# Top-k attention with a feed-forward block: ReLUs of the mask moved to the head of a step, GpSimd's work reordered, more units transposed by VectorE

## The chip, the core and the metric

One core of a Trainium2 chip runs the whole program in one launch. The metric is the device time of that launch in microseconds. Engines are named as in the profile: PE is TensorE (matmuls; PEld are its weight loads), DVE is VectorE, ACT is ScalarE, POOL is GpSimd, SP is SyncE, which issues the DMAs here. Each engine executes its own instructions strictly in the order in which the program has them, and waits on the others by semaphores.

## The reference

```python
# q, k, v: (B=8, H=8, S=576, D=64), float32
scores = q @ k.transpose(0, 1, 3, 2) / 8
kth = np.partition(scores, -32, axis=-1)[..., -32:-31]      # 32nd largest of each row
scores = np.where(scores >= kth, scores, -1e9)
attn = np.exp(scores - scores.max(-1, keepdims=True))
attn = attn / (attn.sum(-1, keepdims=True) + 1e-9)
x = (attn @ v).transpose(0, 2, 1, 3).reshape(8, 576, 512)   # heads side by side

xn = (x - x.mean(-1)) / sqrt(x.var(-1) + 1e-6) * g_ln
out = x + np.maximum(xn @ w_ch1, 0.0) @ w_ch2               # 512 -> 2048 -> 512
```

The two feed-forward weights arrive as 8-byte numbers and are turned into float32 by the kernel itself.

## The kernel before

**Units.** Heads are taken in pairs. For a batch and a head pair, the 576 queries are cut into four tiles of 128 and a rest of 64. A *unit* is one such tile for both heads: two halves of 128 x 576 scores, or, for the rest, one (64 rows of each head). There are 160 units, 20 for each of the 8 batches; 128 are whole, 32 are rests. A *group* is a run of units of one head pair whose products with the values are made together: from batch 2 on, tiles 0, 1 and the rest, then tiles 2 and 3.

**Steps.** The program's main loop has one step for each unit (and a few more at the end). In step `n` it works on several units at once, each at another stage:

- PE makes the scores of unit `n+2` into four PSUM banks (two halves of the keys for two heads, L402), and ACT copies them to SBUF (`scores`, L383, four copies).
- DVE *halves* unit `n+1` at the end of the step (`halve`, L423 and L424: maximum and minimum of the left and right half of a row), so that the top values are sought among 288 columns.
- DVE *selects* in unit `n` (`select`, in four parts): MAX8 finds the 8 largest of each row (L445, L437), MATCH_REPLACE8 takes them out (L431), four times. The eighth value of the fourth time is the threshold.
- For unit `n-1` the mask is made: ACT scales the threshold and the row's maximum (`prepare`, L457 and L458), a very steep ReLU gives a large number where the score is below the threshold (`mask`, L494), POOL subtracts the score from it (L497), and ACT takes Exp with the negative scale and sums the row (`weigh`, L505).
- For unit `n-2` the weights are transposed, so that keys lie on partitions. A *moved* unit goes by DVE: two transposes in 32 x 32 blocks into the unit's score tile (`move`, L536), one DMA to HBM (L551) and, in step `n` = unit + 3, four DMAs back that put the blocks in place (`bring`, L546). Other units go by PE: four transposes for each half (L563), copied out by ACT (L575). The last 64 keys of both heads, the *end keys*, are always transposed by PE (`turn_ends`, L596), for a moved unit in step unit + 3, and copied by ACT (L606).
- Two to four steps behind its last unit, a group is multiplied with the values (`values`, L629 and L636).

**Feed-forward.** When the rows of a batch are ready, a *block* of 256 rows is given to a list of PE work: transposes, hidden layer (L776), projection (L933; the first block's at L815). `fill()`, called some eight times a step, takes as much from that list as the step's share allows; the share is worked out so that a block is finished when the next is given. ACT evacuates (L799, L898, L907), POOL makes sums of the hidden parts (L863 to L869) and of outputs (L913, L917, L747). These run some `fill()` calls later (`sums_later`, `ends_later`, `stores`).

**Weights.** In steps 0 to 20 the weights are converted in 32 pieces, some beforehand, one per step up to step 9, then two: `fetch` (a DMA), `split` (ACT makes magnitude, low part and sign, L163, L165, L168; POOL clamps the magnitude, L164), `shift` (DVE, L176), `join` (POOL, L182 and L184). Up to step 8 a piece is split in the middle of its step; later ones at the end of the step (`weights(n, 1)`). Shift and join come one step later, at its end. After the first block, POOL forms sums of parts of the second weight in four steps (`form_pair`, L987 to L990).

**Watch.** POOL also notes for each unit how far the threshold is from a bound (`watch`, L464), which tells at the end whether a second, slower pass is needed. It reads the unit's halved scores, of which there are two buffers.

**Buffers.** PSUM has two pools: five banks for scores, transposes and products with values, three for the feed-forward. There are five score tiles in SBUF, and two for the masked scores `e`: the ReLU of unit `n-1` writes the one that unit `n-3` had, whose end keys PE must have transposed.

The order on every engine is the order of the calls in the loop; nothing is rearranged.

Of the kernel before, what the change touches and what calls it, by code (L numbers as in the profile page):

```python
# [29 lines left out]
def compute(  # L30
# [31 lines left out]
    HALF = S // 2  # L62
# [35 lines left out]
    def turned():  # L98
        return brief("tp")
# [110 lines left out]
    def weights(n, phase):  # L210

        now, before = batches.get(n, []), batches.get(n - 1, [])
        coming = batches.get(n + 1, [])
        if phase == 0:
            for x in coming if n < LATE else []:
                x.fetch()
            for x in now[0::2] if n < LATE else []:
                x.split()  # L220
        elif phase == 1:
            for x in before:
                x.shift()
            for x in before:
                x.join()
            for x in now if n >= LATE else now[1::2]:
                x.split()
            for x in coming if n >= LATE else []:
                x.fetch()

    todo = []
    share = [0.0]
# [143 lines left out]

    def scores(u):

        u.sc = scpool.tile([P, 2, S], FP32, tag="sc", name="sc")
        made = [score_half(u, s) for s in range(2)]  # L380
        for t in range(len(u.tiles)):
            for s in range(2):
                nc.scalar.copy(  # L383
                    u.sc[:, t, s * HALF : (s + 1) * HALF], made[s][t][:, 0:HALF]
                )

    def score_half(u, s):
# [195 lines left out]
        heads = () if u.moved else range(len(u.tiles))  # L583
        return [lambda t=t: part(t) for t in heads] + [last]

    def turn_ends(u):

        q0 = place_of(u) * 32
        g = u.group
        ps = turned()  # L590
        if u.rest:
            nc.tensor.transpose(ps[0:R, 0:P], u.e[:, 0, JP:S], ident[:])
            nc.tensor.transpose(ps[:, P : 2 * P], u.e[:, 0, JP - R : S], ident[:])
        else:
            ends_e = u.e[:].rearrange("p t n -> p (t n)")[:, JP : JP + P]
            nc.tensor.transpose(ps[:, 0:P], ends_e, ident[:])  # L596

        def copy():
            if u.rest:
                for h in range(2):  # L600
                    nc.scalar.copy(  # L601
                        g.pt[h * R : (h + 1) * R, 2 * J, q0 : q0 + R],
                        ps[h * R : (h + 1) * R, h * (P + R) : h * (P + R) + R],
                    )
            else:
                nc.scalar.copy(g.pt[:, 2 * J, q0 : q0 + P], ps[:, 0:P])  # L606

        return copy
# [443 lines left out]
    CONVERTING = max(n for n in batches if batches[n]) + 2  # L1052
    EARLY = jobs[NHP].first

    for u in units[EARLY:]:
        u.moved = not u.rest and u is not u.group.units[-1]


    for j, after_j in zip(jobs, jobs[1:] + [None]):
# [43 lines left out]
    def at(i):  # L1103
        return units[i] if 0 <= i < N else None
# [94 lines left out]
    nc.sync.dma_start(grow[:], g_ln.rearrange("(c p) -> c p", p=P))  # L1199
    load(fresh[1], nc.sync, nc.scalar)  # L1200
    scores(units[0])
    halve(units[0])
    scores(units[1])
    load_gain()
    weights(-1, 0)
    weights(-1, 1)
    for n in range(END):
# [20 lines left out]
        if quick:  # L1228
            values(g)
            take_values(g)  # L1230
        for x in ahead:
            scores(x)
        if g and not quick:
            values(g)
        if n in brings:
# [14 lines left out]
        if doubt is not None and at(n - 2) and at(n - 2).ends_watch:  # L1250
            settle_watch(at(n - 2).half)
            if n == N + 1:
                tell()
        if early:
            prepare(ex)
            for t in range(2):
                mask(ex, t)
            weights(n, 0)
            for t in range(2):
                weigh(ex, t)  # L1260
        if not early:
            weights(n, 0)
        fill()
        turned_before = at(n - 3)
        if turned_before and turned_before.moved:
            late_ends = turn_ends(turned_before)
        if mk and not early:
            prepare(mk)
            mask(mk, 0)
        fill()  # L1270
        if mk and len(mk.tiles) > 1 and not early:
            mask(mk, 1)
        if g and not quick:
            take_values(g)
        if late_ends:
# [17 lines left out]
                load(fresh[later], nc.sync, nc.sync, n >= EARLY)  # L1293
        if n == 0:
            scores(units[2])
        for x in (u if n < EARLY else None, mk if n > EARLY else None):
            if x and x is units[x.job.last]:
                load_values(x.job)
                ends_due[n + 1] = x.job
# [33 lines left out]
        fill()  # L1333
        if u:
            select(u, 3)
            if doubt is not None:
                watch(u)
        if nxt:
            halve(nxt)
        weights(n, 1)  # L1340
        if g and not quick and g.job.hp == NHP - 1:
            for qt in g.qts:
                if qt < J:
                    arrived(n, (g.job.b, qt), xs[g.job.b, qt])
        if plain_done[0] is not None and plain_done[0] < n:
            if made_pair:
                keep_pair(made_pair.pop())
            if pairs_left:
                made_pair.append(form_pair(pairs_left.pop(0)))
        if late and late.job.hp == NHP - 1:  # L1350
            r = late.job.b // 2
            if r % 2:
# [61 lines left out]
```

## Time and profile before

| | us |
|---|---|
| median of three runs | 1620.12 |
| lowest and highest | 1617.61, 1620.48 |
| the profiled execution | 1619.01 |
| its span, first to last instruction | 1617.1 |

| engine | busy us | share of the span |
|---|---|---|
| PE (PEld beside it) | 1482.7 (1119.5) | 92% (69%) |
| DVE | 1411.5 | 87% |
| ACT | 1072.8 | 66% |
| POOL | 1071.2 | 66% |

The profile is of one execution. It lists busy time by engine and in 40 equal slices (each digit is the busy share in tenths, 9 is 90% or more), groups of instructions by line with their mean duration and the idle time ahead of them, waits ("A <- B" is idle time of A that B's end ended; then the total, how often, and the longest), and the chain of waits, which is followed back from the last instruction. A timeline row has the start, the duration and, in brackets, the idle time ahead and what ended it. A busy PE is not one at its peak, since the ends of matmuls are modelled.

### The profile page before, as it was taken

The page shows a single profiled execution, that of the slowest core. Times are in us where ns is not written, and L with a number is a line of the kernel's source. Part 1 is how long each engine was busy: PE and PEld are TensorE (multiplying, and loading weights), DVE is VectorE, ACT ScalarE, POOL GpSimd, SP SyncE. Part 2 cuts the span into 40 slices and gives each one's busy share as a digit, 9 for nine tenths or more (in the row PEclk, how much of TensorE's full clock was granted, in tenths as well). Part 3 has the DMA queues.
Part 4 walks back from the last instruction along what each step waited for, and adds up shares of the span by engine and source line. Part 5 has one row for each costly group of instructions (what it writes and reads, how often), then busy time and mean ns, then how long its engine had stood idle before and what let it go on. Part 6 is the DMA issues. An engine that isn't in the chain of part 4 may idle for free.

```text
span 1617.1 us, 27069 instructions
## 1 busy us (share of the span) xinstructions
PE 1482.7 (92%) x7770; PEld 1119.5 (69%) x7770; DVE 1411.5 (87%) x3971; ACT 1072.8 (66%) x2984; POOL 1071.2 (66%) x1489
## 2 busy tenths in 40 slices
PE   3568778699979999999999999999999999999997
PEld 1336446467757677777777777777777777778886
DVE  7979888999999999999999999999999999991000
ACT  5877776477767786776766867677667776754221
POOL 6768886766646666677765758576757675746244
PEclk9879999899989999999999999999999999999999
DMA  8424664544646556545564556545555555522211
GB/s 205 123 70 137 174 164 125 156 125 130 182 130 180 154 151 171 161 150 134 163 188 137 140 148 176 162 126 170 146 173 149 136 154 162 164 83 86 73 33 54
DMA packets 367205, 228.27 MB, mean 141 GB/s; under 512 B 248772, under 2 KB 337352, under 8 KB 367048
## 3 DMA queue, kind: packets, MB, share of 16 engines
q1 hardware_dynamic: 362312, 225.86, 49.1%
q8 instruction: 64, 1.05, 0.3%
q10 hardware_dynamic: 4736, 0.59, 0.2%
q14 instruction: 93, 0.76, 0.2%
HBM read 154.01 MB, written 72.35 MB: 140 GB/s over the span
## 4 chain that ended last, share of the span: by engine, by line
PE 70%; POOL 10%; DVE 9%; ACT 6%; DMA 2%; issue 1%; SPq 0%; ACTq 0%; POOLq 0%; DVEq 0%
PE hps L776 26%; PE ops L933 22%; PE scps L402 8%; PE av L629 6%; POOL e L497 3%; DVE m L445 3%; DVE hi L431 2%; PE tp L563 2%; PE av L636 2%; POOL w L184 2%; POOL wt L182 1%; ACT e L494 1%; ACT e L505 1%; ACT sc L383 1%; DVE sc L536 1%
## 5 line engine op out<-in xcount | busy, mean ns | idle before, releaser
L497 POOL TENSOR_TENSOR e<-e,sc 128x576 f32<-128x576 f32 x288 | 417.0, 1466 | 366.9 <-ACT e L494 366.6
L776 PE MATMUL hps<-xT,w 128*128 128x256 f32 x2304 | 550.9, 387 | 13.8 <-ACT xT L738 9.0
L776 PEld LDWEIGHTS hps<-xT,w 128*128 128x128 f32 x2304 | 427.8, 193 | 91.5 <-issue 16.5
L445 DVE MAX8 m<-hi 128x8 f32<-128x296 f32 (+1 forms) x1152 | 469.9, 442 | 0.1
L431 DVE MATCH_REPLACE8 hi<-m,hi 128x288 f32<-128x288 f32 (+1 forms) x864 | 377.2, 441 | 0.0
L933 PE MATMUL ops<-w,h 128*128 128x256 f32 x1360 | 326.0, 384 | 8.9 <-DMA w<-forms 7.8
L505 ACT ACTIVATE e<-e,m 128x576 f32<-128x576 f32 x288 | 224.6, 780 | 129.1 <-POOL e L497 127.6
L933 PEld LDWEIGHTS ops<-w,h 128*128 128x128 f32 x1360 | 250.2, 192 | 52.1 <-issue 8.7
L494 ACT ACTIVATE e<-sc,m 128x576 f32<-128x576 f32 x288 | 211.9, 769 | 91.8 <-PE tp L596 91.5
L383 ACT COPY sc<-scps 128x288 f32<-128x288 f32 x576 | 198.4, 408 | 89.8 <-PE scps L402 57.9
L424 DVE TENSOR_TENSOR lo<-sc 128x576 f32<-128x576 f32 (+1 forms) x160 | 164.9, 1030 | 0.0
L423 DVE TENSOR_TENSOR hi<-sc 128x576 f32<-128x576 f32 (+1 forms) x160 | 154.7, 967 | 8.9 <-ACT sc L383 4.8
L799 ACT ACTIVATE h<-hps 128x512 f32<-128x512 f32 x144 | 85.6, 595 | 96.7 <-PE hps L776 96.2
L629 PE MATMUL av<-pt,vb 128*64 128x256 f32 (+2 forms) x1088 | 142.3, 404 | 2.8 <-ACT pt L601 2.1
L536 DVE STREAM_TRANSPOSE sc<-e 128x512 f32<-128x512 f32 x176 | 114.7, 685 | 31.5 <-POOL e L497 18.9
L933 PE MATMUL ops<-wt,s 128*128 128x256 f32 x544 | 130.1, 381 | 0.0
L402 PE MATMUL scps<-kT,late_qT 64*128 64x288 f32 (+3 forms) x832 | 122.5, 411 | 1.4 <-ACT x L648 1.1
L437 DVE MAX8 hi<-lo 128x8 f32<-128x288 f32 x288 | 117.5, 443 | 0.0
L402 PE MATMUL scps<-kT,qT 64*128 64x288 f32 x512 | 95.1, 467 | 21.5 <-DVE qT L332 11.8
L629 PEld LDWEIGHTS av<-pt,vb 128*64 128x64 f32 x1088 | 72.2, 139 | 59.7 <-issue 12.8
L933 PEld LDWEIGHTS ops<-wt,s 128*128 128x128 f32 x544 | 99.1, 190 | 16.5 <-issue 3.1
L563 PE MATMUL tp<-ident,e 128*128 128x128 f32 x448 | 72.8, 290 | 40.6 <-ACT e L505 40.4
(104 smaller groups left out, 1852.0 us busy)
## 6 DMA issues: line engine op xcount, KB each, us to landing
turned<-sc SPq DMA_DIRECT2D x88, 512.0 KB, 2.9
pt<-turned SPq DMA_DIRECT2D x352, 128.0 KB, 2.8
w<-forms SPq DMA_DIRECT2D x136, 256.0 KB, 4.2
vb<-in_v_dram SPq DMA_DIRECT2D x68, 288.0 KB, 3.9
raw<-in_moe_w_ch_dram SPq DMA_DIRECT2D x32, 512.0 KB, 5.1
kT<-kept SPq DMA_DIRECT2D x36, 288.0 KB, 3.3
kin<-in_k_dram SPq DMA_DIRECT2D x128, 72.0 KB, 2.7
kept<-kT SPq DMA_DIRECT2D x32, 288.0 KB, 3.1
```

The lines of the kernel that those rows point to most:

```text
L383: nc.scalar.copy(u.sc[:, t, s * HALF : (s + 1) * HALF], made[s][t][:, 0:HALF])
L402: nc.tensor.matmul(ps[i * R : i * R + ql, o : o + width], qT[r, q0 : q0 + ql], kT[r, k0 : k0 + width], start=True, stop=True,)
L423: nc.vector.tensor_tensor(hi, a, b, ALU.max)
L424: nc.vector.tensor_tensor(lo, a, b, ALU.min)
L431: nc.vector.match_replace(x, m[:, t, :], x, LOWEST)
L445: nc.vector.max(m[:, t, :], u.hi[:, t, 0:width])
L494: nc.scalar.activation(u.e[:, t], u.sc[:, t], AF.Relu, bias=u.edge[:, t : t + 1], scale=-STEEP)
L497: nc.gpsimd.tensor_tensor(u.e[:, t], u.e[:, t], u.sc[:, t], ALU.subtract)
L505: nc.scalar.activation(u.e[:, t], u.e[:, t], AF.Exp, bias=u.bias[:, t : t + 1], scale=-scale, accum_out=g.den[:, col : col + 1],)
L629: nc.tensor.matmul(av[h * D : (h + 1) * D, 0 : g.nq], vb[:, h * (J + 1) + c, :], g.blocks[:, h, 0 : g.nq // 32, c, :], start=(c == 0), sto ...
L776: nc.tensor.matmul(ps[0][:, side * N : (side + 1) * N], w1[:, c, f * P : (f + 1) * P], self.xT[:, c, 0:N], start=(c == 0), stop=(c == NC - 1),
L933: nc.tensor.matmul(bank[name][:, 0:Q], a(j), rhs, start=first and j == 0, stop=(j == G - 1), skip_group_check=not first,)
```

## The change

In a step's order of calls:

- Shifts of the pieces that were split in the step before stand at the very head. They stood at the end of the step.
- `scores` makes the matmuls alone; the four copies are in `take_scores`, which is called later.
- Directly behind the score matmuls stand the end-key transposes of moved unit `n-3`. They go to columns 288 and following of the first score bank (a bank has 512 columns and a half of scores takes 288), in place of a bank of their own.
- Then come `prepare` and both ReLUs and subtractions of unit `n-1`. They stood behind one and two `fill()` calls (in the first eight units behind the copies).
- Behind the subtractions stand POOL's joins, the watch of unit `n-1` (it was that of unit `n`, at the end of step `n`) and the forming of weight sums (it was at the end of the step).
- Only then are the scores of unit `n+2` copied.

Besides, from batch 2 on the last whole unit of a group without a rest is moved too, unless no group follows: 111 units are moved in the built program, where 88 were.

```diff
         elif phase == 1:
-            for x in before:
-                x.shift()
-            for x in before:
-                x.join()
             for x in now if n >= LATE else now[1::2]:
                 x.split()
...
+    def join_weights(n):
+        for x in batches.get(n - 1, []):
+            x.join()
...
     def scores(u):
 
+        u.made = [score_half(u, s) for s in range(2)]
+        return u.made[0][0][:, HALF:]
+
+    def take_scores(u):
         u.sc = scpool.tile([P, 2, S], FP32, tag="sc", name="sc")
-        made = [score_half(u, s) for s in range(2)]
...
-    def turn_ends(u):
+    def turn_ends(u, ps=None):
...
-        ps = turned()
+        if ps is None:
+            ps = turned()
...
-    for u in units[EARLY:]:
-        u.moved = not u.rest and u is not u.group.units[-1]
+    for j, nj in zip(jobs, jobs[1:] + [None]):
+        for u in units[max(j.first, EARLY) : j.last + 1]:
+            u.moved = not u.rest and (
+                u.i < j.last or (j.b > 1) and nj is not None and not units[nj.first].rest
+            )
...
+        for x in batches.get(n - 1, []):
+            x.shift()
+        spare = None
         for x in ahead:
-            scores(x)
+            spare = scores(x)
+        turned_before = at(n - 3)
+        if turned_before and turned_before.moved:
+            late_ends = turn_ends(turned_before, spare)
+        if mk:
+            prepare(mk)
+            for t in range(len(mk.tiles)):
+                mask(mk, t)
+        join_weights(n)
+        if mk and doubt is not None:
+            watch(mk)
+        if plain_done[0] is not None and plain_done[0] < n - 1:
+            if made_pair:
+                keep_pair(made_pair.pop())
+            if pairs_left:
+                made_pair.append(form_pair(pairs_left.pop(0)))
+        for x in ahead:
+            take_scores(x)
         if g and not quick:
             values(g)
...
+        weights(n, 0)
         if early:
-            prepare(ex)
-            for t in range(2):
-                mask(ex, t)
-            weights(n, 0)
             for t in range(2):
                 weigh(ex, t)
-        if not early:
-            weights(n, 0)
         fill()
-        turned_before = at(n - 3)
-        if turned_before and turned_before.moved:
-            late_ends = turn_ends(turned_before)
-        if mk and not early:
-            prepare(mk)
-            mask(mk, 0)
         fill()
-        if mk and len(mk.tiles) > 1 and not early:
-            mask(mk, 1)
...
             select(u, 3)
-            if doubt is not None:
-                watch(u)
...
-        if plain_done[0] is not None and plain_done[0] < n:
-            if made_pair:
-                keep_pair(made_pair.pop())
-            if pairs_left:
-                made_pair.append(form_pair(pairs_left.pop(0)))
```

More of the change, by code (lines that the diff above doesn't have):

```diff
@@ L210, in weights @@
     def weights(n, phase):
-        now, before = batches.get(n, []), batches.get(n - 1, [])
-        coming = batches.get(n + 1, [])
+        now, coming = batches.get(n, []), batches.get(n + 1, [])
         if phase == 0:
@@ L383, in scores @@
                 nc.scalar.copy(
-                    u.sc[:, t, s * HALF : (s + 1) * HALF], made[s][t][:, 0:HALF]
+                    u.sc[:, t, s * HALF : (s + 1) * HALF], u.made[s][t][:, 0:HALF]
                 )
@@ L1201, in compute @@
     scores(units[0])
+    take_scores(units[0])
     halve(units[0])
     scores(units[1])
+    take_scores(units[1])
     load_gain()
@@ L1295, in compute @@
             scores(units[2])
+            take_scores(units[2])
         for x in (u if n < EARLY else None, mk if n > EARLY else None):
```

## The prediction

> **What bounds the kernel now.** I read the page's head and slices first, then busy time by stage, then single groups, then the timeline. The slices say who is full when:
>
> ```profile
> span 1617.1 us, 27069 instructions
> ...
> PE 1482.7 (92%) x7770; PEld 1119.5 (69%) x7770; DVE 1411.5 (87%) x3971; ACT 1072.8 (66%) x2984; POOL 1071.2 (66%) x1489
> ...
> PE   3568778699979999999999999999999999999997
> ...
> DVE  7979888999999999999999999999999999991000
> ```
>
> No engine is full before slice 10; after it TensorE and VectorE both are, until VectorE runs out of units near 1450 us and TensorE works off the last feed-forward blocks alone. I cut the span at ends of units' selections (units 0, 8, 20, 28, 40, then a batch of 20 units each). Columns: PE, PEld, DVE, ACT, POOL busy (count), clock, DMA share, GB/s.
>
> ```profile
> 21.00:99.00 78.00, 39.60 (x185) 24.73 (x183) 74.71 (x214) 58.53 (x151) 63.10 (x67) 0.85 0.50 136
> 99.00:236.00 137.00, 107.28 (x493) 66.05 (x491) 117.07 (x296) 103.25 (x264) 109.10 (x116) 0.91 0.52 145
> 236.00:329.00 93.00, 74.58 (x361) 52.75 (x362) 79.32 (x212) 51.72 (x147) 68.01 (x83) 0.87 0.48 131
> ...
> 429.00:594.00 165.00, 151.34 (x807) 111.63 (x808) 163.36 (x491) 117.87 (x340) 101.84 (x148) 0.97 0.55 156
> 594.00:765.00 171.00, 168.38 (x927) 128.11 (x924) 170.38 (x500) 126.93 (x366) 119.21 (x171) 1.00 0.55 154
> 765.00:941.00 176.00, 176.00 (x960) 135.85 (x958) 175.45 (x494) 124.96 (x356) 121.88 (x177) 1.00 0.55 155
> ```
>
> From 765 on, TensorE has no gap and VectorE hardly one. They cannot both be the bound by chance, and the halving of the scores shows why they look so (duration is min/median/max, ns):
>
> ```profile
> L423 DVE TENSOR_TENSOR hi<-sc x160: 431/760/1986, 12.0 to 1452.2; 128x576 f32<-128x576 f32 x128, 128x288 f32<-128x288 f32 x32
> L424 DVE TENSOR_TENSOR lo<-sc x160: 443/755/1974, 12.7 to 1452.9; 128x576 f32<-128x576 f32 x128, 128x288 f32<-128x288 f32 x32
> ```
>
> The same instruction takes 0.74 or 1.98 us. Where GpSimd ran nothing beside it, a whole one means 0.746 to 0.749 us; where GpSimd ran all through it, 1.16 (hi) and 1.30 (lo). MAX8 has 0.44 in both cases. Against floors of 0.745 (256 whole ones) and 0.445 (64 of half width), 219 us, the two lines hold 319.6: **100 us of VectorE's busy time is waiting**. By stage: 6.5, 13.0, 7.7, 7.6 in the four before unit 40, 3.4 and 5.8 in the next two batches, then 14 in each of the last four. So in a late batch VectorE needs 176 - 14 = 162 us and TensorE 176: TensorE sets the time, and VectorE is stretched to it. How the stretch comes about, at 871 us:
>
> ```profile
> 870.74 0.78 ACT L494 ACTIVATE e<-sc,m 128x576 f32<-128x576 f32 x1
> ...
> 871.59 2.79 POOL L497 TENSOR_TENSOR e<-e,sc 128x576 f32<-128x576 f32 x2 [1.56 <-ACT e L494]
> ...
> 873.04 1.95 DVE L423 TENSOR_TENSOR hi<-sc 128x576 f32<-128x576 f32 x1
> ...
> 874.33 1.25 POOL L917 TENSOR_TENSOR o<-o,t 128x256 f32<-128x256 f32 x1
> ...
> 874.92 1.27 DVE L424 TENSOR_TENSOR lo<-sc 128x576 f32<-128x576 f32 x1
> ```
>
> TensorE is late, so the score copies and the ReLU behind them are late, so the subtraction falls on the next halving. The waits agree:
>
> ```profile
> POOL e L497 <- ACT e L494: 366.6, 132, 13.0
> ...
> ACT e L494 <- PE tp L596: 91.5, 42, 6.2
> ```
>
> Units 10 to 20 (128 to 236 us) are a third regime: GpSimd is busy 96.1 of 108 us and the chain of waits runs along it without a break:
>
> ```profile
> 175.49 1.66 POOL wt L164 x2
> 177.15 3.10 POOL e L497 x2
> 180.25 0.15 POOL watched L464
> 180.40 1.24 POOL wt L182
> 181.64 0.07 issue
> 181.71 1.27 POOL w L184
> ```
>
> **The change, part by part.** Units turned by VectorE go from 88 to 111 (23 more, in batches 2 to 7; the built program has 46 more transposes, 23 sends and 92 returns).
>
> *Off TensorE:* 8 transposes a unit, 0.44 us for each four in the chain: 0.88 us, 20 us in all. *Off ScalarE:* 46 copies of 0.598, 27.5 us, worth nothing by themselves (66% busy). *On VectorE:* 1.29 us a pair, 30 us. *On SP's queue:* five DMAs a unit, 0.4 + 1.75 us of issuing, 50 us over 900; SP mostly waits, and the keys' rows are needed one step later. Behind them stand the forms' loads (one wait of 7.8 us on them now); price without that cover 0 to 8 us, taken 0.
>
> *Last four batches (15 units).* TensorE bound: 15 x 0.88 = 13, plus what goes with group changes (a four with its switch was 0.54 us in the timeline, so up to 16): **-15**. VectorE needs 162 + 4 x 1.29 = 167 a batch against TensorE's 172, so up to 5 of the 14 us of stretch may stay. Bounds: -20, and +15 if the stretch stays whole (15 x 1.29 = 19, less 4).
>
> *Batches 2 and 3 (8 units, 429 to 765).* VectorE bounds (TensorE 151 of 165, 168 of 171). +8 x 1.29 = 10, less about half of the 9 us of stretch: **+6**, bounds 0 and +10.
>
> *The ReLU at the head.* It no longer waits for four copies (1.3 to 1.5 us) and the fills ahead of it; it still waits for the end-key transpose, now directly behind the scores. So the subtraction moves up 1.5 to 4 us and clears the next halving when TensorE is punctual. Queued behind a waiting ReLU are now the copies; their scores are halved over a step later, and they hold four of five PSUM buffers 1.7 us longer, which the products of values (fifth buffer) and the fills (other banks) cover; uncovered, 1 us in some of 64 steps. Units 0 to 8: the chain runs copies, ReLU, splits, Exp, transposes, scores; 1.4 us of ReLU leaves it each step, but VectorE is busy 74.7 of 78: **-4**, bounds -8 and 0.
>
> *Units 8 to 20.* Shifts go from the end of a step to its head, a step earlier. Now the clamp that a shift needs lands 10 to 14 us after the halving that precedes the new place (unit 12: halving ends at 150.8, clamps at 162.3 and 163.4). So VectorE will stand there, with its selections queued behind; halvings also wait for the watch, now behind the joins. Steps of VectorE, ScalarE and GpSimd then run in lockstep. GpSimd's step: 9.6 us of work now (96.1 / 10) plus 0.3 + 0.8 until the first ReLU is done, 10.7, up to 11.5 with a stretched halving; now it is 10.8. Ten steps: 0 to +7, taken +5. The wait for the first block at 113.8 (5.8 us) shrinks by some 2. Sum **+3**; bounds -20 (all of VectorE's 20 idle us) and +35 (steps of 14).
>
> *Units 20 to 28:* weights are joined nearly a step earlier; TensorE waits 16 us on joins now (L776 4.7, L815 11.1), GpSimd is busy 68 of 93. Half of that and of the 7.7 stretch: **-9**, bounds -18 and 0. *Units 28 to 40:* stretch 7.6, TensorE 94 of 100: **-3**, bounds -6 and +2. The tail is TensorE's own: 0.
>
> *Sum:* -4 + 3 - 9 - 3 + 6 - 15 = **-22**. The profiled execution took 1619.01 (span 1617.1), 1.1 below the median 1620.12; so 1620.1 - 22 = **1598**.
>
> *Weighed against the skill.* The stretched halvings read two SBUF tensors, and only they vary. The Trainium skill (SBUF — State Buffer, Who interferes with whom) says such an instruction contends with a GpSimd instruction that reads SBUF, whoever starts first blocking the other; the rows agree (1.95 under a subtraction). Against the change stands Perfetto Trace Analysis, Identifying the Most-Contended Engine: matmul busy time is no measure of TensorE's headroom, load busy share is, and the busiest other engine is to be relieved. By it VectorE (175.5 of 176) binds and PEld at 136 of 176 leaves room; the 30 us would then come on top, near 1637. The 100 us of stretch within VectorE's busy time is why I don't take it.
>
> **The rivals.** (a) *All stretch goes, and the conversion isn't held:* -8 - 12 - 15 - 6 + 2 - 20 = -59, 1561. For: 100 us of stretch and 43 of idle VectorE before 429 us; against: TensorE's 176 a batch. (b) *The ReLU stays late:* it waits for TensorE anyway (91.5 us), subtractions still fall on halvings; the change does not do its main thing. Half the gain, 1609. (c) *Lockstep in the conversion:* steps of 13 rather than 11.3, ten of them, +17 more, and no gain behind: 1598 + 17 + 9 = 1624. (d) *VectorE sets the pace,* slower: the stretch stays, in place of late subtractions the watch, sums and returned work meet the halvings. Then 23 x 1.29 = +30 stands whole from 429 us on, in place of my -9: 1598 + 39 = 1637. It decides once less than about 14 of the 66 us of stretch behind 429 us are released: 30 - 14, less the 13 of the early stages, leaves +3.
>
> **How the numbers follow.** Forecast 0.42 (own range 1585 to 1608), (a) 0.17, (b) 0.13, (c) 0.13, (d) 0.15. The range, 1562 to 1632, leaves out half of (a) and most of (d). Within 0.2% (3.2 us, about what this measurement can tell from none) lies the edge of (b) and (c): 0.06. Faster 0.74, slower 0.20.
>
> **What would show it.** Right: lines of the halving sum to 250 to 275 us in place of 319; POOL's wait for the ReLU shorter than 367; late batches near 172 with TensorE still at 100%. TensorE with gaps there and VectorE full means (d); VectorE idle before L176 by over 30 us means (c); halvings still above 300 us means (b). I am wrong altogether if batches 2 and 3 grow by more than 10 us each, or if VectorE stands before its halving for the watch in most steps.

## The result and the profile after

| | us |
|---|---|
| before, median of 4 runs beside it (1617.61 to 1622.35) | 1620.3 |
| after, median of 4 runs (1631.43 to 1636.74) | 1633.95 |
| ratio, 95% interval | 1.0084 [1.0065, 1.0103] |
| profiled execution of after, its span | 1633.51, 1631.7 |

The change makes the kernel 14 us slower. The forecast was 22 us faster, and 1633.95 lies 2 us above the range. In the code after the change the lines have moved by two or three: score copies L383 are L385, halves L423 and L424 are L425 and L426, MAX8 L445 is L447, the watch L464 is L466, ReLU L494 is L496, subtraction L497 is L499, Exp L505 is L507, end keys L596 are L599 for moved units, values L629 are L632, oT L644 and xo L671 are L647 and L674.

The head and the slices of the page after, to be laid beside those of before:

```profile
span 1631.7 us, 26871 instructions
...
PE 1477.1 (91%) x7586; PEld 1114.3 (68%) x7586; DVE 1390.1 (85%) x4017; ACT 1034.2 (63%) x2938; POOL 1022.1 (63%) x1489
...
PE   3579678789989899989999999998999999999997
...
DVE  5997978989999999999999999999999999892000
```

Every engine has less busy time than before: VectorE 21 us less although it does 23 units more, GpSimd 49, ScalarE 39, TensorE 6. The time went into waiting. TensorE was not slower at its work: its mean granted clock was 0.959 (0.971 before), and still its two largest groups of matmuls take 386 and 385 ns each on average (387 and 384 before). Behind the twelfth slice TensorE had nines alone before the change, but for the last slice; now there are three eights (slices 14, 18 and 28). Busy time by stage, cut at the same selections as before (PE, PEld, DVE, ACT, POOL, then clock, DMA share, GB/s):

```profile
239.00:322.70 83.70, 61.86 (x299) 45.79 (x300) 76.83 (x210) 48.77 (x135) 64.31 (x78) 0.82 0.46 132
...
426.40:597.50 171.10, 155.25 (x798) 113.87 (x796) 168.58 (x498) 115.27 (x341) 100.58 (x148) 0.94 0.60 170
597.50:769.00 171.50, 166.00 (x870) 126.17 (x868) 170.88 (x507) 118.78 (x352) 107.59 (x170) 0.98 0.62 179
769.00:945.20 176.20, 175.90 (x945) 135.42 (x944) 171.04 (x501) 119.07 (x347) 114.73 (x176) 1.00 0.61 177
945.20:1126.30 181.10, 173.14 (x905) 133.61 (x905) 171.60 (x503) 119.69 (x353) 110.19 (x171) 0.98 0.59 173
```

In the last row neither TensorE (173.1 of 181.1) nor VectorE (171.6) is full: this late batch has 8 us in which TensorE stands and 9.5 in which VectorE does. From the end of unit 80 to that of unit 158 TensorE's gaps are 16.2 us, where they were 2.9. The first unit's selection ends at 27.9 us where it ended at 21.1. All stages (us, spans of the profiled executions; the sum of the differences is, up to rounding, the 14.6 by which the spans differ):

| to the end of unit | 0 | 8 | 20 | 28 | 40 | 80 | 158 | tail |
|---|---|---|---|---|---|---|---|---|
| before | 21.1 | 77.9 | 137.3 | 92.5 | 99.7 | 336.0 | 687.8 | 164.7 |
| after | 27.9 | 72.8 | 138.3 | 83.7 | 103.7 | 342.6 | 697.4 | 165.4 |
| difference | +6.8 | -5.1 | +1.0 | -8.8 | +4.0 | +6.6 | +9.6 | +0.7 |

The halving, duration as min/median/max in ns, and what it waited for:

```profile
L425 DVE TENSOR_TENSOR hi<-sc x160: 430/739/1806, 11.1 to 1472.2; 128x576 f32<-128x576 f32 x128, 128x288 f32<-128x288 f32 x32
...
  POOL watched L466: 57.7, 36
```

L425 and L426 hold 261.8 us (129.7 and 132.1) where L423 and L424 held 319.6. The 58 us by which the halving got shorter stand in the next line again: VectorE now waits 57.7 us (4.0 before) for the watch before it halves. That exchange is a part of the loss; the runs below price it. Other waits of the kernel after:

```profile
POOL e L499 <- ACT e L496: 384.0, 97, 12.9
...
ACT e L496 <- PE scps L599: 95.6, 74, 3.8
...
ACT sc L385 <- POOL e L499: 48.3, 24, 7.0
```

GpSimd waits longer for the ReLU than before (384 against 367 us), the ReLU a little longer for the end keys (95.6 against 91.5), and ScalarE's score copies now wait for subtractions. How a late batch loses TensorE's time is read from two engines' timelines at 1108 us (start, duration, idle time ahead in brackets):

```profile
1107.52 1.44 ACT L496 ACTIVATE e<-sc,m 128x576 f32<-128x576 f32 x2
1113.05 1.31 ACT L385 COPY sc<-scps 128x288 f32<-128x288 f32 x4 [4.09 <-DMA turned<-sc]
1114.22 0.42 ACT L647 COPY oT<-av 128x256 f32<-128x256 f32 x1
```

```profile
1107.77 2.97 PE L936 MATMUL ops<-wt,s 128*128 128x256 f32 x13
1114.69 0.44 PE L674 MATMUL xo<-ident,oT 128*128 128x128 f32 x2 [3.95 <-ACT oT L647]
```

ScalarE stands before the score copy until a moved unit's transfer has left the score tile that the copy is to fill; behind it in ScalarE's order stands the copy of the values' product (L647), and for that TensorE stands 3.95 us. A unit that is moved holds its score tile until its transfer has landed; with 23 more of them the score copies stand for this 20 times, where it was 5 times before.

### The profile page after: what moved, and what is told of

It is laid out like the page before. It is cut to its first block, busy times and chain, and to the rows that moved or that the text cites. A ratio compares the mean times of both kernels' runs of the same rounds, so it can differ in the third digit from the quotient of the medians.

```text
span 1631.7 us, 26871 instructions
## 1 busy us (share of the span) xinstructions
PE 1477.1 (91%) x7586; PEld 1114.3 (68%) x7586; DVE 1390.1 (85%) x4017; ACT 1034.2 (63%) x2938; POOL 1022.1 (63%) x1489
## 3 DMA queue, kind: packets, MB, share of 16 engines
q8 instruction: 63, 1.03, 0.3%
## 5 line engine op out<-in xcount | busy, mean ns | idle before, releaser
L499 POOL TENSOR_TENSOR e<-e,sc 128x576 f32<-128x576 f32 x288 | 406.5, 1430 | 439.1 <-ACT e L496 384.0
L779 PE MATMUL hps<-xT,w 128*128 128x256 f32 x2304 | 539.2, 386 | 5.1 <-ACT xT L741 2.9
L779 PEld LDWEIGHTS hps<-xT,w 128*128 128x128 f32 x2304 | 436.4, 194 | 73.5 <-issue 7.7
L447 DVE MAX8 m<-hi 128x8 f32<-128x296 f32 (+1 forms) x1152 | 469.4, 442 | 0.1
L936 PE MATMUL ops<-w,h 128*128 128x256 f32 x1360 | 321.2, 385 | 4.5 <-DMA w<-forms 4.2
L936 PEld LDWEIGHTS ops<-w,h 128*128 128x128 f32 x1360 | 257.3, 194 | 40.8 <-DMA w<-forms 4.3
L496 ACT ACTIVATE e<-sc,m 128x576 f32<-128x576 f32 x288 | 209.3, 768 | 97.5 <-PE scps L599 95.6
L507 ACT ACTIVATE e<-e,m 128x576 f32<-128x576 f32 x288 | 228.1, 795 | 31.9 <-POOL e L499 30.9
L385 ACT COPY sc<-scps 128x288 f32<-128x288 f32 x576 | 187.2, 404 | 80.9 <-POOL e L499 48.3
L425 DVE TENSOR_TENSOR hi<-sc 128x576 f32<-128x576 f32 (+1 forms) x160 | 129.7, 811 | 61.6 <-POOL watched L466 57.7
L538 DVE STREAM_TRANSPOSE sc<-e 128x512 f32<-128x512 f32 x222 | 143.6, 682 | 21.5 <-ACT e L507 10.9
L632 PE MATMUL av<-pt,vb 128*64 128x256 f32 (+2 forms) x1088 | 144.4, 408 | 4.3 <-DMA pt<-turned 2.4
L426 DVE TENSOR_TENSOR lo<-sc 128x576 f32<-128x576 f32 (+1 forms) x160 | 132.1, 825 | 0.0
L632 PEld LDWEIGHTS av<-pt,vb 128*64 128x64 f32 x1088 | 73.9, 140 | 54.2 <-issue 3.7
L404 PEld LDWEIGHTS scps<-kT,late_qT 64*128 64x128 f32 (+1 forms) x832 | 71.0, 169 | 58.5 <-issue 19.5
```

The costliest lines, as they stand in the source:

```text
L385: nc.scalar.copy(u.sc[:, t, s * HALF : (s + 1) * HALF], u.made[s][t][:, 0:HALF])
L404: nc.tensor.matmul(ps[i * R : i * R + ql, o : o + width], qT[r, q0 : q0 + ql], kT[r, k0 : k0 + width], start=True, stop=True,)
L426: nc.vector.tensor_tensor(lo, a, b, ALU.min)
L447: nc.vector.max(m[:, t, :], u.hi[:, t, 0:width])
L496: nc.scalar.activation(u.e[:, t], u.sc[:, t], AF.Relu, bias=u.edge[:, t : t + 1], scale=-STEEP)
L499: nc.gpsimd.tensor_tensor(u.e[:, t], u.e[:, t], u.sc[:, t], ALU.subtract)
```

## The experiments

The theory after the result: the losses are (1) 23 moved units, which hold score tiles longer, (2) the watch early, on which the halving waits, (3) the shifts at the head, which hold the first selections. The rival is the prediction's own account (TensorE sets the late batches, so moved units gain and something in the order eats it). Ratios are to the kernel before, run on the same chip beside each set; its medians there were 1618.1, 1618.7, 1620.2, 1619.5 and 1619.6. All kernels below are the kernel after with pieces taken back, unless they are called before with something added.

### The order alone, the moved units alone

`order_only` has the new order with the old rule for moved units (88); `moved_only` is the kernel before with the new rule (111):

```diff
-    for j, nj in zip(jobs, jobs[1:] + [None]):
-        for u in units[max(j.first, EARLY) : j.last + 1]:
-            u.moved = not u.rest and (...)
+    for u in units[EARLY:]:
+        u.moved = not u.rest and u is not u.group.units[-1]
```

> The new order of calls alone, with the 88 moved units of before. Theory A (new waits): the order brings waits that cost as much as it releases (57 us of halvings that wait for the watch, shifts at the head, copies behind the subtraction); only 30 us of VectorE transposes go, so 1622 to 1630. Theory B (the extra moved units are the whole loss): the order is the gain that was forecast, 1595 to 1610.

> The kernel before with the 23 more units moved, nothing else. Theory A: about neutral, 1615 to 1628, since TensorE loses 20 us of transposes and VectorE gains 30 of which the stretch of its halvings gives back part. Theory B: the loss is here, 1633 or more, with VectorE at 100% and gaps on TensorE.

Measured: `order_only` 1626.41, 1.0056 [1.0038, 1.0074], as theory A had it; `moved_only` 1642.5, 1.015 [1.0131, 1.0169], as theory B had it. The moved units alone cost 24 us, near the 23 x 1.29 = 30 us that they put on VectorE, and nothing of TensorE's saving shows. A late batch of `moved_only`:

```profile
773.90:952.40 178.50, 175.74 (x945) 133.60 (x942) 177.95 (x502) 119.97 (x346) 123.52 (x178) 1.00 0.60 175
952.40:1136.00 183.60, 174.33 (x912) 133.44 (x913) 183.05 (x504) 123.55 (x355) 118.54 (x171) 0.98 0.59 172
```

VectorE is full (183.05 of 183.60), TensorE has 9 us of gaps, and the halvings still hold 315.5 us. TensorE has room here and the stretch is the same: a late TensorE is not what makes it. That VectorE's added work is the loss isn't shown by this run alone, since ScalarE's score copies wait far longer for the transfers of moved units, before and in `moved_only`:

```profile
ACT sc L383 <- DMA turned<-sc: 11.1, 5, 2.9
```

```profile
ACT sc L383 <- DMA turned<-sc: 85.3, 32, 7.6
```

The runs with 111 units and the spare columns, below, part the two. In `order_only` the order alone costs 8 us. By stage of its profiled execution (4 us longer than that of before), 7 us are lost before the first selection ends (28.3 against 21.1), units 0 to 28 gain 14, and units 28 to 158 lose 10.

### The watch back at the end; the score copies ahead of the ReLUs

`watch_end` puts the watch of unit `n` back behind its selection; `copies_first` copies the scores ahead of `prepare` and the ReLUs:

```diff
-        if mk and doubt is not None:
-            watch(mk)
...
             select(u, 3)
+            if doubt is not None:
+                watch(u)
```

```diff
+        for x in ahead:
+            take_scores(x)
         if mk:
             prepare(mk)
...
-        for x in ahead:
-            take_scores(x)
```

> The changed kernel with the watch back at the end of its own unit's step. Theory A: the halving's wait for the watch falls from 57 us to under 10, the stretch of the halvings rises by 10 to 25 us since GpSimd stands again until the threshold is there; 1615 to 1628. Rival: these waits only mirror a late TensorE, which sets the time anyway; 1631 to 1637.

> The changed kernel with the four score copies ahead of the scaling and the ReLUs again (still no fill between). Theory A: ScalarE's copies no longer wait for the subtraction (48 us to 0), TensorE's waits for oT and for score copies (33 us together) halve, the ReLU starts 1.5 us later; 1620 to 1630. Rival (ScalarE's order does not matter): 1631 to 1637.

Measured: `watch_end` 1625.59, 1.0035 [1.0016, 1.0055], 8 us faster than after, as theory A had it. Its halvings hold 291.6 us, 30 more than in after, and VectorE's idle time in a late batch is 0.5 us where it was 5 to 10. The halving is stretched again under the subtraction, and still this is the cheaper way. `copies_first` 1672.61, 1.0326 [1.0292, 1.036], 39 us slower than after, which neither expectation had: its score copies wait 109.9 us (37 times) for transfers of moved units, against 20.0 (20 times) in after. The ReLUs ahead of the copies give a transfer time to land.

### Shifts back at the end; the end keys in a bank of their own

`shift_end` puts shifts and joins back to the end of the step. `ends_first` turns the end keys ahead of the score matmuls into their own bank, held until the copy at L609. `order_fixed` and `all_fixed` take the watch, the shifts and the end keys back together, with 88 and 111 units.

```diff
-        for x in batches.get(n - 1, []):
-            x.shift()
...
-        join_weights(n)
...
+        for x in batches.get(n - 1, []):
+            x.shift()
+        join_weights(n)
         weights(n, 1)
```

```diff
-        spare = None
-        for x in ahead:
-            spare = scores(x)
         turned_before = at(n - 3)
         if turned_before and turned_before.moved:
-            late_ends = turn_ends(turned_before, spare)
+            late_ends = turn_ends(turned_before)
+        for x in ahead:
+            scores(x)
```

> The changed kernel with shifts and joins back at the end of the step behind the split. Theory A (each new wait has its own price): the first unit's selection, 28 us into the changed kernel and 21 into the one before, is back near 21, VectorE's waits for clamps fall from 23 us to under 10; 1622 to 1629. Rival (the conversion is GpSimd's own time wherever the shifts stand): 1630 to 1637.

> The changed kernel with the end-key transposes ahead of the score matmuls, into a bank of their own. In the changed kernel TensorE takes 234 ns from the start of such a transpose to the next matmul, 109 ns in the kernel before. Theory A: 107 x 0.125 = 13 us of TensorE and a ReLU that is released 1.3 us earlier, so the halving's wait for the watch falls from 57 to about 40; 1618 to 1628. Rival (TensorE has room, VectorE's own time decides): 1630 to 1636.

> The new order with the 88 units of before, and three places undone: watch, shifts and joins at the end of the step, end-key transposes ahead of the scores. What stays of the change: prepare, ReLUs and subtractions at the head of the step, ahead of the score copies. Theory A: 7 us at the start, 6 to 8 from the watch, 5 to 13 from TensorE: 1598 to 1612, faster than the kernel before. Rival (moving the ReLUs up is worth nothing in itself): 1616 to 1624.

> The same with the 111 moved units of the change. Theory A: VectorE's 30 us of transposes come on top and TensorE has 20 us less, so 5 to 15 above the one with 88 units: 1606 to 1620. Rival (once the waits are gone the moved units pay): at or below the one with 88.

Measured: `shift_end` 1623.51, 1.0036 [1.0023, 1.0049], 10 us faster than after, as theory A had it; its first selection ends at 20.5 us. Shifts and joins go back together, and no run parts them. Why the shifts at the head hold the first selection, VectorE in the kernel after:

```profile
14.34 0.43 DVE L176 TENSOR_SCALAR size<-size 128x512 uint32<-128x512 uint32 x1 [1.77 <-POOL size L164]
...
17.89 0.76 DVE L176 TENSOR_SCALAR size<-size 128x512 uint32<-128x512 uint32 x2 [3.13 <-POOL size L164]
...
19.85 0.43 DVE L176 TENSOR_SCALAR size<-size 128x512 uint32<-128x512 uint32 x1 [1.20 <-POOL size L164]
```

Four shifts of the first pieces stand ahead of the selection of unit 0 and wait 1.8 + 3.1 + 1.2 us for clamps that GpSimd has only begun; the selection, for which everything is there, is queued behind them.

`ends_first` 1682.38, 1.0405 [1.036, 1.045], 48 us slower than after, which neither expectation had. A wait of 86 us appears, for a score copy, before the matmuls with the values:

```profile
PE av L632 <- ACT sc L385: 86.4, 32, 9.3
```

Four scores and the end keys hold all five banks of the pool, so the values' product gets one only when a score has been copied, and the copies stand behind the ReLUs. Nor was much of TensorE's time won: an end-key transpose ahead of the scores still takes 203 ns to the start of the next matmul (16 of them in units 80 to 100). `order_fixed` 1646.97, 1.0188 [1.0157, 1.0218], and `all_fixed` 1670.81, 1.0329 [1.03, 1.0358], carry the same wait (58.7 and 89.7 us), so they miss both of their expectations and say nothing about the watch and the shifts together. With end keys in a bank of their own, ReLUs ahead of the copies cost more than they bring.

### With the spare columns kept

`kept` (88 units) and `kept_111` take back the watch and the shifts and leave the end keys in the spare columns. `shift_88` takes back only the shifts, with 88 units. `spare_only` is `kept` with the late ReLUs of before:

```diff
-        if mk:
+        if mk and early:
             prepare(mk)
             for t in range(len(mk.tiles)):
                 mask(mk, t)
...
         fill()
+        if mk and not early:
+            prepare(mk)
+            mask(mk, 0)
         fill()
+        if mk and len(mk.tiles) > 1 and not early:
+            mask(mk, 1)
```

> The kernel before with three things of the change kept (ReLUs ahead of the score copies, end keys in the spare columns, joins' place behind them) and three undone: 88 units turned by transfers, the watch at the end of its own unit's step, shifts and joins at the step's end. Theory (the losses of the change are separate and add): the changed order with 88 units took 1626.4; the watch's return was worth 8.4 us and the return of the shifts 10.4 us where each was undone alone, so 1626.4 - 8.4 - 10.4 = 1608, 0.993 of before, with the first batch's end back near 21 us and VectorE waiting under 10 us for the watch. Rival (the watch and the shifts cost the same wait on GpSimd, and the halves are drawn out again once the watch no longer holds VectorE): 1615 to 1619, 0.998 to 1.0, with the halves near 320.

> The same as the run with everything kept, but with the change's 111 units turned by transfers. If the 23 units cost in this order what they cost between the two runs of the changed order (1634 against 1626.4), it is 1616, level with before; if they cost as in the old order, where VectorE set the pace (+24), it is 1630 or more. Forecast of the prediction's TensorE account: below the run with 88 units by 4 to 20 us.

> The changed order with the watch in its new place, 88 units, and only the shifts and joins back at the step's end. Theory of separate losses: 1626.4 - 10.4 = 1616, 0.998 of before, halves below 280 and a wait of VectorE for the watch of 60 to 80 us. Rival (the watch early is a gain once the startup is mended): 1608 or less.

> As the run with everything kept, but the mask's ReLUs stand where they stood before, behind the values: of the change, the spare columns for the end keys alone are left. Theory (the gain is the ReLU's early place, the spare columns only make it possible): 1616 to 1622, level with before, halves near 320, the stages of units 0 to 28 as in before. Rival (TensorE sets the late batches, so that the transposes' 18 us count by themselves): 1600 to 1606.

Measured: `kept` 1610.44, 0.9937 [0.9922, 0.9953]; `kept_111` 1614.19, 0.9958 [0.9943, 0.9974]; `shift_88` 1616.06, 0.9974 [0.9964, 0.9985]; `spare_only` 1610.54, 0.9939 [0.992, 0.9959]. The losses of the watch and of the shifts are separate, or nearly: the sum for `kept` was 1608, and `kept_111` and `shift_88` came out at the 1616 of their theories, within 2 us. Halvings hold 316.9 us in `kept`, as much as before, although its ReLUs stand at the head; with the watch early (`shift_88`) they hold 266.7 and VectorE waits 90.6 us for the watch. So it is the watch, not the ReLU, that takes the halving off the subtraction: the watch stands behind the subtraction on GpSimd, the halving behind the watch, and VectorE stands for as long as it was slowed before, and longer. `spare_only` fell between the two expectations: the ReLU's early place is worth nothing with 88 units, yet the kernel is 10 us faster than before with three things of the change left in it. In the profiled executions units 0 to 28 gain 17 us and units 28 to 158 lose 9. (Its second expectation was badly put: with 88 units TensorE has no transposes less than before.)

### What the 10 us are, and what the ReLU's place is worth

`spare_alone` is before with the spare columns only, `early_relus` before with the ReLUs of the units that TensorE turns (the first eight; the text on record calls them 16) ahead of the score copies, `pairs_only` before with the weights' pairs formed early in the step. `spare_111` is `spare_only` with 111 units.

`scores` is the function of after, which makes the matmuls alone:

```diff
         for x in ahead:
             scores(x)
+        if mk and early:
+            prepare(mk)
+            for t in range(len(mk.tiles)):
+                mask(mk, t)
+        for x in ahead:
+            take_scores(x)
```

> Late ReLUs, spare columns and 111 units turned by transfers. If the ReLUs ahead of the score copies are what covers the copies' wait for a transfer: 1626 to 1636, 16 us or more over the same kernel with 88 units (1610.5), with some 80 us of waits of ScalarE's score copies for transfers. If it is the spare columns: 1612 to 1618, with 10 to 25 us of such waits.

> The kernel before with the end keys turned into the spare columns behind the score matmuls, and nothing else of the change but the joins' and copies' functions. If the spare columns bring the 10 us: 1609 to 1612. If the early units' ReLUs or the pairs do: 1617 to 1622; the stage of units 0 to 8 is then 78 and that of units 8 to 20 near 137, as before.

> The kernel before with the ReLUs of its first 16 units (those turned by TensorE) ahead of the score copies, and nothing else. If these bring the gain of units 8 to 20: 1609 to 1613, with that stage near 127; if the pairs or the spare columns do, 1618 to 1622.

> The kernel before with the pairs of the weights formed behind the scores, early in the step, and nothing else. If the pairs' early place brings the gain: below 1614, in units 20 to 28. Otherwise 1618 to 1622, and a pair formed early holds a bank of the scores for a step, so up to 5 us may be lost.

Measured: `early_relus` 1611.73, 0.9962 [0.9948, 0.9977]; `pairs_only` 1617.52, 0.9989 [0.9976, 1.0003]; `spare_alone` 1622.54, 1.0026 [1.001, 1.0043]; `spare_111` 1634.9, 1.0101 [1.0084, 1.0118]. The gain is mostly the first eight ReLUs': 7.7 us against 2.0 for the pairs, which is within the noise, and the spare columns alone lose 3. Units 8 to 20 take 130.9 us in `early_relus` (137.3 before; 127 was expected). One step holds it: the one behind the end of unit 8's selection, where the first block's rows are normalised, takes 14.0 us where it took 20.1. VectorE's waits in this step, before and in `early_relus`:

```profile
DVE st L699 <- ACT x L648: 5.8, 1, 5.8
DVE den L1241 <- ACT den L517: 2.2, 1, 2.2
```

```profile
DVE st L702 <- ACT x L651: 2.9, 1, 2.9
```

The weights of unit 7 are ready earlier, and with them the whole chain of transposes, values and rows that VectorE stood for.

`spare_111` settles the other question. Without the ReLUs at the head the 23 units cost 24.4 us (1634.9 against 1610.5), as in the old order; with them 3.8 (1614.2 against 1610.4). The waits of ScalarE's score copies, in `spare_111` and in `kept_111`:

```profile
ACT sc L385 <- DMA turned<-sc: 61.4, 24, 6.0
```

```profile
ACT sc L385 <- DMA turned<-sc: 15.6, 14, 4.0
```

So the head place of the ReLUs is worth 21 us with 111 units and nothing with 88, where these waits are 11.8 us without it and none with it. The reading is that it fills the time in which a transfer must land. VectorE's wait for the watch falls as well, from 18.2 to 4.6 us, and may have a part. VectorE makes the same 222 transposes in both kernels, so its added work alone is not what cost 24 us in the old order.

### The parts that gain, together

`early_pairs` is before with the first eight ReLUs and the pairs early, and nothing else.

> The kernel before with the two parts of the change that gained by themselves, and nothing else: the first eight units' ReLUs ahead of the score copies (units 0 to 7, which TensorE turns; an earlier text calls them the first 16) and the weights' pairs early in the step. If the two gains are separate (7.7 and 2.0 us against the kernel before of the same call): 1607 to 1611, below every other version, since the late batches keep the 688 us that they had before where the versions with end keys in the spare columns have 693. If the pairs cost a bank that the late batches need: 1612 to 1616.

Measured: 1608.32, 0.9928 [0.9912, 0.9944]. It is the fastest version by its median, though `kept` (0.9937) lies within its interval; the gains add (7.7 + 2.0 expected, 11.3 measured, and the interval is some 2.6 us wide to either side). The late batches did not keep the 688 us of the expectation: units 80 to 158 take 690.3.

## Why the prediction was wrong

The step that failed is the largest term of the sum, -15 for the last four batches: it took what the moved units save TensorE for time of the kernel, and put TensorE's waits at nothing. The change from before to after, as a chain of runs; the first step has three things in it, and each later one differs from the one ahead in one thing (medians; the kernel before varies by 2 us between the sets):

| step | us | to |
|---|---|---|
| first eight ReLUs, pairs, spare columns (`spare_only`) | -9.7 | 1610.5 |
| 23 more moved units (`spare_111`) | +24.4 | 1634.9 |
| the other ReLUs at the head (`kept_111`) | -20.7 | 1614.2 |
| the watch behind the subtractions (`shift_end`) | +9.3 | 1623.5 |
| shifts at the head, joins behind the subtractions (after) | +10.4 | 1634.0 |

The three things of the first step come to -7.7, -2.0 and +3.1 by themselves (`early_relus`, `pairs_only`, `spare_alone`), 3 us short of what they bring together; this is as wide as the noise.

**The premise, "100 us of VectorE's busy time is waiting", with TensorE setting the late batches: half right.** With 88 units it holds. VectorE has 29 us less work in units 80 to 158 of `shift_88` than of `kept` (654.1 against 683.1), TensorE has no gap to speak of in either (1.8 us), and the stretch takes the same time (692.9 and 692.6). The halvings of after gave back what was forecast, too: VectorE has 171 to 172 us of work in a whole late batch, where the sum had 167 and up to 5 of stretch. But how late TensorE is does not decide how far the halving is stretched: with gaps on TensorE the halvings hold 315.5 us (`moved_only`), and with an early ReLU and 88 units 316.9 (`kept`). Where the watch takes the halving off the subtraction, VectorE waits for the watch instead.

**Last four batches, -15: +9.6.** TensorE's busy time in units 80 to 158 fell by 3.7 us (684.9 to 681.2), and its gaps grew by 13.3 (2.9 to 16.2). The moved units did take 10.6 us off TensorE there (680.2 in `kept_111`, 690.8 in `kept`), where 13 was forecast for 15 of them, and 2 for group changes. Against this the end keys cost TensorE more behind the scores: from the start of such a transpose to that of the next matmul it takes 234 ns on average (17 of them in units 80 to 100) where it took 109, and TensorE's part is 690.1 us in `spare_alone`, in which they alone have moved, 5 more than before. The gaps are the term that the sum hasn't got. Of the 16 us in after, 5.2 are waits for a score copy and 10.1 waits for the copy of a values' product; the timeline above shows such a copy behind score copies that wait for a transfer. Late batches of `kept` (first row) and `kept_111`:

```profile
748.30:924.80 176.50, 176.50 (x957) 136.15 (x956) 175.95 (x493) 122.45 (x354) 120.81 (x177) 1.00 0.54 154
...
756.20:931.40 175.20, 175.20 (x945) 134.48 (x941) 174.65 (x502) 118.86 (x346) 120.89 (x176) 1.00 0.61 179
931.40:1111.00 179.60, 173.75 (x909) 133.67 (x906) 179.05 (x504) 119.89 (x353) 117.83 (x171) 0.98 0.60 175
```

In `kept_111` VectorE is full again, though its halvings gave back 18 us over the whole kernel (298.7 against 316.9), and the 10.6 us freed on TensorE stand as 11.8 us of gaps: units 80 to 158 take 692.0 us with 111 units and 692.6 with 88. So, by one profiled execution of each, the +9.6 is 4.8 from before to `kept` (`spare_alone` has 4.9, by the end keys alone), -0.6 for the moved units, and 5.4 from there to `shift_end` and after (697.4 in both) for the watch, for which VectorE waits 27.9 us in these units of after. The bound on the bad side, +15, held.

**Batches 2 and 3, +6: +6.6.** Right, but VectorE and the copies' waits share it.

**The ReLU at the head.** That the scores hold four of five PSUM buffers 1.7 us longer, and that products of values and fills cover this, failed in part: TensorE waits 37 us in after for a bank that a score copy frees (the largest part, 17.4, ahead of the transposes of a block's rows, L738), where before it was 6.5; 14 of them lie in batches 2 and 3, 5 in the last four batches. That it clears the next halving failed (316.9 against 315.9 us in `kept` and `spare_only`; with 111 units 298.7 against 302.0). What it is worth, 21 us of cover for transfers, the prediction had not seen; it took a moved unit's transfer for a matter of SP's queue, price 0 to 8 us, and did not ask how long the score tile is held. **Units 0 to 8, -4: -5.1**, right in size and in part by luck: `early_relus` takes 2.0 us off this stage, and the rest comes with the late start, for in `shift_end`, which starts in time, the stage is 0.9 shorter than before. At the end of unit 8 after is 1.6 us behind the kernel before. The same edit brings 6 us in the step after them.

**Units 8 to 20, +3: +1.0.** Right in size by luck, since two misses cancel. The stage takes 127.6 us in `shift_end`, so the place of shifts and joins costs 10.7 in after where 5 was forecast, and the rest of the change brings 9.7 where 2 was forecast, 6.4 of them by the first eight ReLUs (`early_relus`). In after VectorE waits 23.5 us ahead of its shifts over the whole conversion (9.5 before), 6.1 of them before the first selection. **Units 20 to 28, -9: -8.8**, right in size and half in reason: the stage takes 87.0 us in `pairs_only` (92.5 before), 87.8 in `shift_end` and 83.7 in after, so the pairs' early place brings some 5 and the earlier shifts and joins 4; the prediction had the joins and the stretch. **Units 28 to 40, -3: +4.0**, failed: the halvings gave back 5.5 us here (23.0 to 17.5), and the stage still got longer. TensorE is busy 99.1 of its 103.7 us, where it was 94.1 of 99.7 (in units 20 to 28 it has 12.7 less to do than before), and VectorE waits 9.2 us for the watch. **The start, taken at nothing: +6.8.** The prediction looked for the price of the shifts at the head in units 8 to 20 and not at the first step, where four pieces are shifted at once.

**The rivals.** 1637 for "VectorE sets the pace" was nearest, by luck: its condition, less than 14 us of stretch released behind 429 us, was not met (40 us were released in units 40 to 158, 226.9 to 186.8), and the 23 units that it prices at 30 us cost 3.8 with the ReLUs at the head. `moved_only` has its picture, VectorE full and the stretch whole, and the wait for transfers beside it. That the watch would meet the halvings was rightly named there, as a contention; it came as a wait. Of the signs named ahead, halvings of 250 to 275 us came true (261.8) and misled. GpSimd's wait for the ReLU grew (384 us), late batches did not come near 172, and VectorE stood before its halving for the watch in 36 of 160 steps, not in most; the 23.5 us ahead of the shifts stay under the 30 that stood for lockstep.

**The rule that the prediction weighed.** The rule of the Trainium skill (Perfetto Trace Analysis, Identifying the Most-Contended Engine), by which VectorE binds and TensorE has room, would have given the right sign. The runs show it only in part: with 6 to 8 us less work on VectorE in each late batch (`shift_88`, 88 units) TensorE still has no gap and units 80 to 158 take 692.9 us, as in `kept` with VectorE full (692.6). So at 88 units TensorE had no room, with weight loads at 136 of 176 us; and with 10.6 us less on TensorE (`kept_111`) VectorE had none.

Not settled: by how much the wait for transfers would fall with a sixth score tile; it was not tried. Nor do the runs tell how much of TensorE's gaps in after comes from the wait for transfers and how much from VectorE, which waits for the watch.

## What to carry to other kernels

When two engines are both full, ask of an instruction that seems stretched what it would wait for if it were not: here the halving met the subtraction in either way, as contention or as a wait, and the wait was dearer. Moving work to a transfer also makes its source tile busy until the transfer lands; look for the next writer of that tile, and for what stands behind that writer in its engine's order. A bundle of edits is best priced edit by edit: here the new place of shifts and joins lost 10 us, that of the first eight ReLUs gained 8, and the fastest version keeps two small edits.

## What the runs showed of the hardware

- What a transpose of the end keys holds of TensorE depends on its neighbours. Between two feed-forward matmuls it takes 109 ns to the start of the next matmul (before); behind the score matmuls 164 to 166 ns when a feed-forward matmul follows, and 256 to 260, once 586, when the values' matmul does (after, units 80 to 100). Its weight load waits for nothing that the profile shows (30.3 us over 78 of them in after).
- A DVE instruction that reads two SBUF tensors of 128x576 means 0.75 us where GpSimd runs nothing beside it, and takes up to 1.99 us under GpSimd's work (before); MAX8, which reads one, has 0.44 us in both cases. To let it wait for the subtraction's end instead saved 50 us of its busy time (316.9 to 266.7) and cost 84 us of waiting (6.6 to 90.6), for 5.6 us of time (`kept` against `shift_88`).
